# Fused attention and two MLPs on one core: in the last three head pairs, GpSimd forms one of four low parts of the transposed exponentials from an SBUF copy, and late raw weights may lie in weight slots

## The chip, the cores and the metric

One core of a Trainium2 chip runs the whole program. The metric is the device time of one execution in microseconds (us); lower is better. Engine names as in the profile: PE is TensorE (PEld its weight loads), DVE VectorE, ACT ScalarE, POOL GpSimd, SP the queue that issues DMAs.

## The reference

```python
# q, k, v: (4 batches, 8 heads, 576 positions, 64)
scores = (rot(q) @ rot(k).T) / 8
attn = exp(scores - scores.max(-1)); attn /= attn.sum(-1) + 1e-9
x = (attn @ v).transpose(0, 2, 1, 3).reshape(2304, 512)
r = maximum(x @ w_in, 0)                       # w_in 512 x 2048
x = (s * (r * r) + b) @ w_out                  # w_out 2048 x 512
g = x @ w_gate                                 # 512 x 1536
out = (g / (1 + exp(-g)) * (x @ w_val)) @ w_out2
```

The weights arrive as 64-bit floats; the output is float32.

## The kernel before, in words

Matmuls keep float32 precision by splitting both operands into a high part (rounded to fp32r) and a low part (the rest). Three matmuls make one product: high by high, high by low, low by high (L874, L875, L876).

**Attention** runs over 16 head pairs p = 0 to 15. A pair's query axis is cut into nine units u of 128 rows and three thirds y of three units each. For a unit, PE makes scores `ps_s` (L677), DVE the negated maximum `nm` (L680), ACT the exponentials `e` (L684). For a third, PE transposes `e` into PSUM in four parts i = 0 to 3 (`ps_t`, L740; the last, 64 rows high, L743). In each part ACT writes the high half `ph` from PSUM (L748), and DVE the low half as `ps_t - ph` (`pl`, L755; for part 3 the low half lies in rows 64 to 127 of `ph`). PE then multiplies by the values (`ps_av`, L770 with `ph`, L772 with `pl`) and ACT evicts the result to `xr` (L783). POOL splits the values into `vh` (L627 high, L629 low); the second half of a pair's values has to wait until `ps_av` no longer reads the old one.

**MLPs.** Weights come as 512 KB tiles `raw` (SP, L305 and L307). A tile holds two chunks, and each is decoded to float32 by four instructions: `dec` on ACT (L323), then on DVE L326, L329 and L334. ACT rounds the high half `w` (L364), POOL or DVE subtracts for the low half (L371). A decoded `dec` is also stored to DRAM (`up`, L349), since later token blocks read it back (L1141) and combine several pieces on DVE (L1155, L1163) for a product with fewer multiplications (`hb`, `acc`). The first MLP's work on batch 0 begins while the last pairs of attention still run, and fills PE between their matmuls. The decode of its weights lies on the same engines as the attention's splitting.

**Order.** Every instruction is handed to a planner inside the kernel as `op(engine, estimated time, function, priority, needs, tokens taken, tokens given back)`. A token stands for a buffer of a pool. The planner runs a list schedule with these estimates and emits each engine's instructions in that order; on the chip each engine runs its list strictly in order. So one edit of an operation can move others, on all engines. `third(y)` in `pair(p)` emits the parts named above, `load()` and the decode functions the weights. The transposes and the `ps_av` groups keep their own order among themselves (`in_turn`).

Of the kernel before, what the change touches and what calls it, by code (L numbers as in the profile page):

```python
# [8 lines left out]
F32 = mybir.dt.float32  # L9
F32R = mybir.dt.float32r  # L10
U32 = mybir.dt.uint32
AF = mybir.ActivationFunctionType
ALU = mybir.AluOpType
# [139 lines left out]
def t_act(n, psum=True, aps=0):  # L153
    return 0.833e-3 * n + (0.051 if psum else 0.093) + 0.093 * aps


def t_dve(n, aps=0):
    return n / 960.0 + 0.065 + 0.06 * aps
# [6 lines left out]
def t_pool(n):  # L165
    return 2.35e-3 * n + 0.08


def t_pool1(n):
    return 1.1e-3 * n + 0.08  # L170
# [7 lines left out]
def tile_attention_moe_moe(  # L178
# [43 lines left out]
    WU0 = 63  # L222
    WUS = 7
    QP = 11

    sch = Schedule()
    op = sch.op
# [63 lines left out]
    def fetch(key, prio, dep=None, after=(), acq=()):  # L291

        kind, f = key
        src = {"in": w_in, "out": w_out, "gate": w_gate, "val": w_val, "out2": w_out2}[kind]
        wide = src.dtype != F32
        n = 2 if wide else 1
        if wide:
            src = src.bitcast(U32)
        st = {}
        raw_tok = Token("raw")  # L300

        def load():
            st["raw"] = raw = raw_p.tile([128, n * 512], U32 if wide else F32, tag="raw", name="raw")
            if kind in ("out", "out2"):
                nc.sync.dma_start(out=raw, in_=src[f * 128:(f + 1) * 128, :])  # L305
            else:
                nc.sync.dma_start(  # L307
                    out=raw.rearrange("p (k m) -> p k m", k=KD),
                    in_=src[:, f * 128 * n:(f + 1) * 128 * n].rearrange("(k p) m -> p k m", p=128),
                )  # L310

        o = W_ld[key] = sch.dma(n * 262144, load, prio, (dep,), (raw_tok, *acq), after=after, pace=1.5)
        if wide:
            dec_tok = Token("dec", "wb") if kind == "in" and f >= WA // 2 else Token("dec")

            def d0():
                two = st["raw"].rearrange("p (m two) -> p m two", two=2)
                st["low"], st["high"] = two[:, :, 0], two[:, :, 1]
                if dec_tok.pool == "dec":
                    st["t"] = dec_p.tile([128, 512], U32, tag="dec", name="dec")  # L320
                else:
                    st["t"] = late[dec_tok.pool].tile([128, 2, 512], F32R, tag="w", name="dec")[:, 0].bitcast(U32)
                nc.scalar.activation(out=st["t"].bitcast(F32), in_=st["high"].bitcast(F32), func=AF.Copy, scale=2.0 ** -112)  # L323

            def d1():
                nc.vector.tensor_scalar(out=st["t"], in0=st["t"], scalar1=3, scalar2=None, op0=ALU.logical_shift_left)  # L326

            def d2():
                nc.vector.scalar_tensor_tensor(  # L329
                    out=st["t"], in0=st["high"], scalar=0x80000000, in1=st["t"], op0=ALU.bitwise_and, op1=ALU.bitwise_or  # L330
                )

            def d3():
                nc.vector.scalar_tensor_tensor(  # L334
                    out=st["t"], in0=st["low"], scalar=29, in1=st["t"], op0=ALU.logical_shift_right, op1=ALU.bitwise_or
                )
                st["val"] = st["t"].bitcast(F32)

            o = op("act", t_act(512, False), d0, prio, (o,), (dec_tok,))
            o = op("dve", t_dve2(512), d1, prio, (o,), port=True)  # L340
            o = op("dve", t_dve(512), d2, prio, (o,), port=True)
            o = op("dve", t_dve(512), d3, prio, (o,), (), (raw_tok,), port=True)
            end = (dec_tok,)
        else:
            st["val"] = None
            end = (raw_tok,)
        if kind != "out":
            dst = {"in": lambda: w_pair["up", f // 2][f % 2], "gate": lambda: w_pair["gv", f][0], "val": lambda: w_pair["gv", f][1], "out2": lambda: w_last_d[f]}[kind]
            kept[key] = sch.dma(262144, lambda: nc.sync.dma_start(out=dst(), in_=st["raw"] if st["val"] is None else st["val"]), prio, (o,), (), end, pace=1.2)  # L349
        return st, o, end  # L350
# [294 lines left out]
    def pair(p, st):  # L645
# [78 lines left out]
        def third(y, pr):  # L724
# [2 lines left out]
            need, give = [exps[u] for u in us] + [eye_op], [e_tok[u] for u in us]  # L727
            ph_tok, pl_tok = Token("ph"), Token("pl")
            blocks = [(u, kc) for kc in range(4) for u in us]
            done = {}  # L730
            for i in range(4):
                t_tok = Token("t")
                part = blocks[4 * i:4 * i + 4]
                n, rows = (512, 128) if part else (QT, 64)

                def tr(i=i, part=part):
                    ps = st["pt", y, i] = ps_t.tile([128, 512], F32, tag="t", name="ps_t")
                    if part:
                        for z, (u, kc) in enumerate(part):
                            nc.tensor.transpose(ps[:, z * 128:z * 128 + 128], st["e", u][:, kc * 128:kc * 128 + 128], ident)  # L740
                    else:
                        for z, u in enumerate(us):
                            nc.tensor.transpose(ps[0:64, z * 128:z * 128 + 128], st["e", u][:, 512:S], ident)  # L743

                def hi(i=i, n=n, rows=rows):
                    if i == 0:
                        st["ph", y] = ph_p.tile([128, 4 * QT + QT], F32R, tag="ph", name="ph")
                    nc.scalar.activation(out=st["ph", y][0:rows, 512 * i:512 * i + n], in_=st["pt", y, i][0:rows, 0:n], func=AF.Copy)  # L748

                def lo(i=i, n=n, rows=rows):  # L750
                    if i == 0:
                        st["pl", y] = pl_p.tile([128, 4 * QT], F32R, tag="pl", name="pl")
                    c = slice(512 * i, 512 * i + n)
                    dst = st["pl", y][:, c] if rows == 128 else st["ph", y][64:128, c]
                    nc.vector.tensor_tensor(out=dst, in0=st["pt", y, i][0:rows, 0:n], in1=st["ph", y][0:rows, c].bitcast(F32), op=ALU.subtract)  # L755

                o = op("pe", 0.11 * (len(part) or 3), tr, pr + 8 * i, need, (t_tok,), give)
                in_turn(o)
                o = op("act", t_act(n), hi, pr + 8 * i, (o,), (ph_tok,) if i == 0 else ())
                done[i] = op("dve", t_dve(n), lo, pr + 8 * i, (o,), (pl_tok,) if i == 0 else (), (t_tok,))  # L760
            v_tok, tmp = Token("v"), Token("tmp")
            o = None
            spans = ((0, 0, QT),) if y == 0 else ((0, 0, QT // 2), (1, QT // 2, QT)) if y == 1 else ((1, 0, QT),)
# [265 lines left out]
    def x_load_s(i):  # L1029
# [28 lines left out]
        for name, home, kh, th, names, zs in quads:  # L1058
            mine = []
            for o, m, b, s in x_pieces(t0 + QS * th, QS, S):  # L1060
                def ld(home=home, kh=kh, o=o, m=m, b=b, s=s, names=names, zs=zs):
                    if o == 0:
                        take(names, zs)
                    for h in range(2):
                        nc.sync.dma_start(
                            out=half(st[home][h])[:, :, o:o + m].bitcast(F32),
                            in_=x_d[b].rearrange("(k p h) t -> h p k t", h=2, p=128)[h, :, 2 * kh:2 * kh + 2, s:s + m],
                        )
                x = sch.dma(2 * 1024 * m, ld, prio, deps, (*(y for x in names for y in toks[x]), *(v_tok[y] for y in zs)) if o == 0 else (), after=lds[-1:])
                x.dur = 1.1  # L1070
                lds.append(x)
                mine.append(x)
            r_tok = r_toks[name] = Token(*ALL)
            for y, (o, m, b, s) in enumerate(x_pieces(t0 + QS * th, QS, S)):
                def ld(name=name, kh=kh, o=o, m=m, b=b, s=s, y=y, r_tok=r_tok):
                    if y == 0:
                        st["r", name] = flat(r_tok).bitcast(F32)[:, 0:n]
                    for j in range(2):
                        src = r_d[b][2 * kh:2 * kh + 2, S * j + s:S * j + s + m]
                        nc.sync.dma_start(  # L1080
                            out=half(st["r", name])[64 * j:64 * j + 64, :, o:o + m],
                            in_=bass.AP(src.tensor, src.offset, [[0, 64], *(list(x) for x in src.ap)]),
                        )
                x = sch.dma(1024 * m, ld, prio, deps, (r_tok,) if y == 0 else (), after=lds[-1:])
                x.dur = 1.1
                lds.append(x)
                mine.append(x)
            need[name] = mine
# [594 lines left out]
```

## Time and profile before

| | |
|---|---|
| median of 3 runs | 1091.49 us (1089.80 to 1091.75) |
| profiled execution | 1093.18 us, its span 1091.40 us |
| busy, share of the span | PE 1076.0 us (99%), PEld 976.4 (89%), DVE 886.2 (81%), ACT 737.0 (68%), POOL 225.3 (21%) |

The profiled execution has its own time: 1.78 us lie outside the span, and it is 1.69 us above the median of the runs that were timed without a profile. Attention holds the first 289 us of the span; from then on only the MLPs run. A matmul counts as busy until its modelled end, so a high share is not PE at its peak.

### The profile page before, as it was taken

How to read it: one execution, taken by the hardware profiler on the slowest of the kernel's cores; microseconds unless marked ns; L12 is line 12 of the kernel's file. 1: busy time of each engine (PE TensorE's matmuls, PEld its weight loads, DVE VectorE, ACT ScalarE, POOL GpSimd, SP SyncE). 2: the span in 40 equal slices, each digit the busy share in tenths (PEclk: the TensorE clock that was granted, in tenths of full speed). 3: DMA queues.
4: the chain of work that ended last, by engine and by line, in shares of the span. 5: the costliest groups of instructions: out<-in, count | busy, mean ns of one | idle time of the engine just before them, and what ended most of it. 6: DMA issues, size and time to landing. Idle time of an engine off the chain costs nothing.

```text
span 1091.4 us, 17609 instructions
## 1 busy us (share of the span) xinstructions
PE 1076.0 (99%) x6188; PEld 976.4 (89%) x6188; DVE 886.2 (81%) x1560; ACT 737.0 (68%) x1511; POOL 225.3 (21%) x197
## 2 busy tenths in 40 slices
PE   8999999999999999999999999999999999999998
PEld 7899988998888899999888888999989999899996
DVE  6999999999888998879999998876596675966751
ACT  5998999999887876646665556655565554655550
POOL 7898778983210000000000000000000000000000
PEclk8999999999999999999999999999999999999999
DMA  4666868656569555472556654312331122311102
GB/s 124 199 186 226 269 185 260 192 187 206 147 209 271 152 174 174 140 228 88 172 184 202 227 170 148 123 62 65 89 95 39 59 68 80 97 48 45 53 2 57
DMA packets 111192, 155.51 MB, mean 142 GB/s; under 512 B 34416, under 2 KB 67200, under 8 KB 111104
## 3 DMA queue, kind: packets, MB, share of 16 engines
q1 hardware_dynamic: 110288, 153.60, 44.9%
q8 instruction: 49, 0.80, 0.3%
q10 hardware_dynamic: 816, 0.79, 0.2%
q14 instruction: 39, 0.32, 0.1%
HBM read 99.98 MB, written 32.58 MB: 121 GB/s over the span
## 4 chain that ended last, share of the span: by engine, by line
PE 86%; DVE 5%; ACT 4%; DMA 3%; issue 1%; SPq 0%; DVEq 0%; ACTq 0%
PE hb L874 14%; PE hb L876 14%; PE hb L875 14%; PE ps_s L677 6%; PE acc L876 5%; PE acc L875 5%; PE acc L874 5%; PE acc L1465 5%; PE acc L1466 5%; PE acc L1464 5%; PE ps_t L740 4%; PE ps_av L770 3%; PE ps_av L772 2%; DVE nm L680 2%; ACT e L684 1%; DVE pl L755 1%
## 5 line engine op out<-in xcount | busy, mean ns | idle before, releaser
L874 PE MATMUL hb<-w 128*128 128x384 f32 (+1 forms) x728 | 250.9, 345 | 0.0
L876 PE MATMUL hb<-w 128*128 128x384 f32 (+1 forms) x728 | 250.5, 344 | 0.0
L875 PE MATMUL hb<-w 128*128 128x384 f32 (+1 forms) x728 | 250.1, 344 | 0.0
L874 PEld LDWEIGHTS hb<-w 128*128 128x128 f32 x728 | 136.7, 188 | 9.2 <-ACT tmp L1267 0.6
L875 PEld LDWEIGHTS hb<-w 128*128 128x128 f32 x728 | 136.7, 188 | 7.4
L876 PEld LDWEIGHTS hb<-w 128*128 128x128 f32 x728 | 136.7, 188 | 4.6
L680 DVE TENSOR_REDUCE nm<-ps_s 128x1 f32<-128x576 f32 x144 | 107.9, 751 | 9.4 <-PE ps_s L677 7.6
L748 ACT ACTIVATE ph<-ps_t 128x512 fp32r<-128x512 f32 x192 | 106.0, 570 | 11.0 <-PE ps_t L740 9.8
L684 ACT ACTIVATE e<-ps_s,nm 128x576 f32<-128x576 f32 x144 | 107.3, 745 | 8.5 <-DVE nm L680 7.3
L876 PE MATMUL acc<-gh,w 128*128 128x512 f32 (+1 forms) x288 | 106.8, 371 | 0.0
L875 PE MATMUL acc<-gl,w 128*128 128x512 f32 (+1 forms) x288 | 106.7, 370 | 0.0
L874 PE MATMUL acc<-gh,w 128*128 128x512 f32 (+1 forms) x288 | 106.6, 370 | 0.0
L677 PE MATMUL ps_s<-t,a 128*128 128x288 f32 x320 | 100.8, 331 | 4.3 <-ACT e L684 3.7
L770 PE MATMUL ps_av<-ph,vh 128*128 128x384 f32 (+1 forms) x320 | 97.1, 333 | 2.2 <-DVE ph L755 1.3
L755 DVE TENSOR_TENSOR pl<-ps_t,ph 128x512 fp32r<-128x512 f32 x144 | 95.6, 682 | 2.3 <-ACT ph L748 1.0
L1525 ACT ACTIVATE tmp<-hb 128x384 f32<-128x384 f32 x144 | 70.4, 489 | 34.5 <-PE hb L876 32.7
L677 PE MATMUL ps_s<-kz,a 128*128 128x288 f32 x320 | 90.5, 298 | 0.0
L740 PE MATMUL ps_t<-ident,e 128*128 128x128 f32 x576 | 85.9, 274 | 2.9 <-DVE pl L755 1.2
L740 PEld LDWEIGHTS ps_t<-ident,e 128*128 128x128 f32 x576 | 68.6, 141 | 10.0 <-issue 1.7
L1163 DVE TENSOR_TENSOR w<-sums,w 128x512 fp32r<-128x512 f32 x104 | 68.2, 684 | 7.7 <-ACT w L1161 7.5
L772 PE MATMUL ps_av<-pl,vh 128*64 128x384 f32 (+1 forms) x256 | 72.4, 295 | 0.0
L677 PEld LDWEIGHTS ps_s<-t,a 128*128 128x128 f32 x320 | 61.6, 192 | 9.9 <-ACT e L684 8.2
(139 smaller groups left out, 2430.3 us busy)
## 6 DMA issues: line engine op xcount, KB each, us to landing
raw<-gv SPq DMA_DIRECT2D x36, 512.0 KB, 3.7
raw<-in_moe_w_out_dram SPq DMA_DIRECT2D x28, 512.0 KB, 4.6
x_d<-xr SPq DMA_DIRECT2D x64, 144.0 KB, 3.0
raw<-in_moe_w_in_dram SPq DMA_DIRECT2D x16, 512.0 KB, 4.5
raw<-up SPq DMA_DIRECT2D x16, 512.0 KB, 3.9
raw<-in_moe_w_gate_dram SPq DMA_DIRECT2D x12, 512.0 KB, 4.6
raw<-in_moe_w_val_dram SPq DMA_DIRECT2D x12, 512.0 KB, 5.0
gv<-dec SPq DMA_DIRECT2D x24, 256.0 KB, 2.6
```

The costliest lines, as they stand in the source:

```text
L677: nc.tensor.matmul(ps[:, hf * 512:hf * 512 + HS], a[:, q0:q0 + 128], m[:, k0:k0 + HS], start=y == 0, stop=y == len(todo) - 1)
L680: nc.vector.tensor_reduce(out=st["nm"][:, u:u + 1], in_=st["s", u], axis=AX.XY, op=ALU.max, negate=True)
L684: nc.scalar.activation(out=st["e", u].rearrange("p (f n) -> p f n", f=2), in_=st["s", u], func=AF.Exp, bias=st["nm"][:, u:u + 1], accum_ou ...
L740: nc.tensor.transpose(ps[:, z * 128:z * 128 + 128], st["e", u][:, kc * 128:kc * 128 + 128], ident)
L748: nc.scalar.activation(out=st["ph", y][0:rows, 512 * i:512 * i + n], in_=st["pt", y, i][0:rows, 0:n], func=AF.Copy)
L755: nc.vector.tensor_tensor(out=dst, in0=st["pt", y, i][0:rows, 0:n], in1=st["ph", y][0:rows, c].bitcast(F32), op=ALU.subtract)
L770: nc.tensor.matmul(ps, vv, st["ph", y][:, c], start=kc == 0, stop=kc == 4, skip_group_check=True)
L772: nc.tensor.matmul(ps[0:64], vv[:, 0:64], st["pl", y][:, c], start=False, stop=False, skip_group_check=True)
L874: nc.tensor.matmul(o, lh, rh, start=first, stop=False, skip_group_check=more)
L875: nc.tensor.matmul(o, lh, rl, start=False, stop=False, skip_group_check=more)
L876: nc.tensor.matmul(o, ll, rh, start=False, stop=last, skip_group_check=more)
L1525: nc.scalar.activation(out=st[key, f], in_=ps[name], func=AF.Copy)
```

## The change

1. For pairs 13, 14 and 15 (`LP = 13`), part i = 0 of each third (`LC = (0,)`) is split in another way. ACT copies `ps_t` from PSUM to an SBUF tile `raw` (a slot of the later `gl` buffers, token "gb"), and the `ps_t` buffer is given back when that copy ends, not after DVE's subtraction. POOL rounds the copy to `ph` (`hi_p`) and subtracts to `pl` (`lo_p`). DVE's subtraction is left out. These are nine parts of 128x512. The other three parts of a third stay as they were.
2. `raw` tiles of the first MLP's weights with f of at least `WA // 2` may take a slot of the weight buffers ("wb") where no "raw" slot is free.
3. Some loads of a later block carry `pace=1.3` in the planner's account. That alters its estimate, not the transfer.

```diff
+    LP = 13
+    LC = (0,)
...
-        raw_tok = Token("raw")
+        raw_tok = Token("raw", "wb") if kind in ("in", "out") and f >= WA // 2 else Token("raw")
...
-            st["raw"] = raw = raw_p.tile([128, n * 512], U32 if wide else F32, tag="raw", name="raw")
+            if raw_tok.pool == "raw":
+                st["raw"] = raw = raw_p.tile([128, n * 512], U32 if wide else F32, tag="raw", name="raw")
+            else:
+                st["raw"] = raw = late["wb"].tile([128, 2, 512], F32R, tag="w", name="raw").rearrange("p h m -> p (h m)").bitcast(U32)
...
+                def copy(i=i):
+                    if i == 0:
+                        both()
+                    st["raw", y, i] = late["gb"].tile([128, 512], F32R, tag="gl", name="raw").bitcast(F32)
+                    nc.scalar.activation(out=st["raw", y, i], in_=st["pt", y, i], func=AF.Copy)
+
+                def hi_p(i=i):
+                    c = slice(512 * i, 512 * i + 512)
+                    nc.gpsimd.tensor_scalar(out=st["ph", y][:, c], in0=st["raw", y, i], scalar1=1.0, scalar2=0.0, op0=ALU.mult, op1=ALU.add)
+
+                def lo_p(i=i):
+                    c = slice(512 * i, 512 * i + 512)
+                    nc.gpsimd.tensor_tensor(out=st["pl", y][:, c], in0=st["raw", y, i], in1=st["ph", y][:, c].bitcast(F32), op=ALU.subtract)
+
                 o = op("pe", 0.11 * (len(part) or 3), tr, pr + 8 * i, need, (t_tok,), give)
                 in_turn(o)
-                o = op("act", t_act(n), hi, pr + 8 * i, (o,), (ph_tok,) if i == 0 else ())
-                done[i] = op("dve", t_dve(n), lo, pr + 8 * i, (o,), (pl_tok,) if i == 0 else (), (t_tok,))
+                first = (ph_tok, pl_tok) if i == 0 else ()
+                begun = None if i == 0 else act_op[0]
+                if p >= LP and i in LC:
+                    r_tok = Token("gb")
+                    o = act_op[i] = op("act", t_act(n), copy, pr + 8 * i, (o, begun), (*first, r_tok), (t_tok,))
+                    o = op("pool", t_pool1(n), hi_p, pr + 8 * i, (o,))
+                    done[i] = op("pool", t_pool(n), lo_p, pr + 8 * i, (o,), (), (r_tok,))
+                    continue
+                o = act_op[i] = op("act", t_act(n), hi, pr + 8 * i, (o,), first)
+                done[i] = op("dve", t_dve(n), lo, pr + 8 * i, (o,), (), (t_tok,))
...
-                x = sch.dma(2 * 1024 * m, ld, prio, deps, ..., after=lds[-1:])
+                x = sch.dma(2 * 1024 * m, ld, prio, deps, ..., after=lds[-1:], pace=1.3 if i == 1 else 1.0)
```

The lists of all engines are the same up to about 246 us of the profiled execution of before. From there they differ until about 470 us, where PE's list is the same again. The diff adds lines: L684 of before is L689 after, L680 is L685, L748 is L758, L755 is L763, L364 is L369, L371 is L376, L627 and L629 are L632 and L634, L770 and L772 are L800 and L802; L769 is the new copy, L773 and L777 are `hi_p` and `lo_p`.

The first three places are at the start of pair 13's tail, from 246 us on. ACT's list there, before and then after; `w` with `dec` is the rounding of a weight:

```order
L684 ACTIVATE e_3905,l_3470<-ps_s_3861,nm_3730 128x576
L748 ACTIVATE ph_3915<-ps_t_3896 128x512
L684 ACTIVATE e_3925,l_3470<-ps_s_3888,nm_3730 128x576
L748 ACTIVATE ph_3915<-ps_t_3910 128x512
L748 ACTIVATE ph_3915<-ps_t_3929 128x512
L364 ACTIVATE w_3950<-dec_3721 128x512
L783 ACTIVATE xr_3783<-ps_av_3884 128x384
L684 ACTIVATE e_3963,l_3470<-ps_s_3920,nm_3730 128x576
```

```order
L689 ACTIVATE e_3905,l_3470<-ps_s_3861,nm_3730 128x576
L769 ACTIVATE raw_3917<-ps_t_3896 128x512
L689 ACTIVATE e_3927,l_3470<-ps_s_3888,nm_3730 128x576
L758 ACTIVATE ph_3915<-ps_t_3910 128x512
L758 ACTIVATE ph_3915<-ps_t_3931 128x512
L689 ACTIVATE e_3953,l_3470<-ps_s_3922,nm_3730 128x576
L813 ACTIVATE xr_3783<-ps_av_3884 128x384
L758 ACTIVATE ph_3915<-ps_t_3957 64x384
```

The copy to `raw` stands in the place of the first `ph`. The rounding of the weight, which stood ahead of the eviction `xr`, has gone back four rows, and an exponential stands in its place.

DVE's list at the same place, before and then after; `dec` is the decode of a weight:

```order
L680 TENSOR_REDUCE nm_3730<-ps_s_3888 128x1
L334 SCALAR_TENSOR_TENSOR dec_3721<-raw_3286,dec_3721 128x512
L755 TENSOR_TENSOR pl_3937<-ps_t_3896,ph_3915 128x512
L680 TENSOR_REDUCE nm_3730<-ps_s_3920 128x1
L755 TENSOR_TENSOR pl_3937<-ps_t_3910,ph_3915 128x512
L755 TENSOR_TENSOR pl_3937<-ps_t_3929,ph_3915 128x512
L680 TENSOR_REDUCE nm_3730<-ps_s_3944 128x1
```

```order
L685 TENSOR_REDUCE nm_3730<-ps_s_3888 128x1
L339 SCALAR_TENSOR_TENSOR dec_3722<-raw_3287,dec_3722 128x512
L685 TENSOR_REDUCE nm_3730<-ps_s_3922 128x1
L763 TENSOR_TENSOR pl_3916<-ps_t_3910,ph_3915 128x512
L763 TENSOR_TENSOR pl_3916<-ps_t_3931,ph_3915 128x512
L685 TENSOR_REDUCE nm_3730<-ps_s_3946 128x1
```

One subtraction, that of part 0, is gone; the rest has moved up by a row.

POOL's list there, before and after; `vh` is the split of values, `w` the low half of a weight:

```order
L371 TENSOR_TENSOR w_3894<-dec_3613,w_3894 128x512
L627 TENSOR_SCALAR vh_3959<-vr_3636 128x5x64
L371 TENSOR_TENSOR w_3950<-dec_3721,w_3950 128x512
L629 TENSOR_TENSOR vh_3959<-vr_3636,vh_3959 128x5x64
L627 TENSOR_SCALAR vh_4092<-vr_3636 128x5x64
```

```order
L376 TENSOR_TENSOR w_3894<-dec_3613,w_3894 128x512
L773 TENSOR_SCALAR ph_3915<-raw_3917 128x512
L777 TENSOR_TENSOR pl_3916<-raw_3917,ph_3915 128x512
L632 TENSOR_SCALAR vh_3974<-vr_3636 128x5x64
L634 TENSOR_TENSOR vh_3974<-vr_3636,vh_3974 128x5x64
L773 TENSOR_SCALAR ph_3979<-raw_3981 128x512
L777 TENSOR_TENSOR pl_3980<-raw_3981,ph_3979 128x512
L376 TENSOR_TENSOR w_4000<-dec_3722,w_4000 128x512
```

Each copy brings two POOL instructions, and they stand ahead of the next split of values. Over the tail of attention, ACT's list holds nine weight instructions (L323, L364 of before) where it held twelve, and DVE's thirteen decode instructions where it held seventeen; the others come behind it.

SP's list at the end of attention, before and after; `x_d3` and `up` are stores, `raw` loads:

```order
L305 DMA raw_4648<-in_moe_w_out_dram 128x1024
L307 DMA raw_4701<-in_moe_w_in_dram 128x4x256
L349 DMA up3_141<-dec_4698 128x512
L305 DMA raw_4738<-in_moe_w_out_dram 128x1024
L307 DMA raw_4778<-in_moe_w_in_dram 128x4x256
L349 DMA up4_142<-dec_4750 128x512
```

```order
L312 DMA raw_4732<-in_moe_w_in_dram 128x4x256
L310 DMA raw_4740<-in_moe_w_out_dram 128x1024
L312 DMA raw_4746<-in_moe_w_in_dram 128x4x256
L310 DMA raw_4751<-in_moe_w_out_dram 128x1024
L312 DMA raw_4757<-in_moe_w_in_dram 128x4x256
L310 DMA raw_4766<-in_moe_w_out_dram 128x1024
```

Before, a store of a decoded tile stands between every two loads. After, the loads follow one another, eleven in a row, since weight slots take them.

## Rows read from the trace of the kernel before

**Rows 1.** Busy time of each engine in four stretches of the span.

```profile
core 0: us, PE busy (x) PEld busy (x) DVE busy (x) ACT busy (x) POOL busy (x), PEclk, DMA share, GB/s
27.00:246.00 219.00, 214.12 (x1675) 199.11 (x1674) 205.18 (x326) 205.46 (x487) 184.79 (x154) 1.00 0.67 213
246.00:289.00 43.00, 40.60 (x303) 35.83 (x302) 42.06 (x71) 41.05 (x97) 12.85 (x14) 1.00 0.57 173
289.00:379.00 90.00, 90.00 (x408) 73.78 (x408) 79.29 (x124) 72.49 (x124) 7.95 (x6) 1.00 0.70 215
379.00:1064.00 685.00, 684.79 (x3515) 628.29 (x3514) 540.37 (x1007) 400.41 (x767) 0.00 (x0) 1.00 0.35 113
```

**Rows 2.** The chain that ended last, 240 to 292: start, us, engine, line.

```profile
251.56 0.83 ACT e L684 x2
...
266.45 0.67 DVE pl L755
...
285.97 0.55 DVE ph L755
```

**Rows 3.** PE's timeline: start, us, line, tiles, shapes [idle before <-releaser].

```profile
248.04 0.34 PE L677 MATMUL ps_s<-t,a 128*128 128x288 f32 x1
248.21 0.30 PE L677 MATMUL ps_s<-kz,a 128*128 128x288 f32 x1
...
249.94 0.41 PE L770 MATMUL ps_av<-ph,vh 128*128 128x384 f32 x1 [0.65 <-ACT xr L783]
...
286.57 0.44 PE L770 MATMUL ps_av<-ph,vh 128*128 128x384 f32 x1 [0.81 <-DVE ph L755]
```

**Rows 4.** Waits, 246 to 289: us in total, times, longest us.

```profile
PEld ps_s L677 <- ACT e L684: 1.3, 4, 0.5
PEld ps_av L770 <- DVE ph L755: 1.2, 1, 1.2
```

**Rows 5.** Groups of instructions, 246 to 289: count, busy us, mean ns, idle before.

```profile
L755 DVE TENSOR_TENSOR pl<-ps_t,ph 128x512 fp32r<-128x512 f32 x24 | 15.9, 681 | 0.3 <-ACT ph L748 0.2
L748 ACT ACTIVATE ph<-ps_t 128x512 fp32r<-128x512 f32 x25 | 14.3, 594 | 0.9 <-PE ps_t L740 0.9
...
L371 POOL TENSOR_TENSOR w<-dec,w 128x512 fp32r<-128x512 f32 x6 | 7.7, 1283 | 11.5 <-DVE pl L755 7.3 <-ACT w L364 4.2
...
L783 ACT ACTIVATE xr<-ps_av 128x384 f32<-128x384 f32 x8 | 4.0, 496 | 0.1
...
L334 DVE SCALAR_TENSOR_TENSOR dec<-raw,dec 128x512 uint32<-128x512 uint32 x5 | 3.4, 680 | 0.0
...
L364 ACT ACTIVATE w<-dec 128x512 fp32r<-128x512 f32 x5 | 3.2, 638 | 0.3 <-DVE dec L334 0.3
```

**Rows 6.** POOL's groups over the whole run.

```profile
L627 POOL TENSOR_SCALAR vh<-vr 128x320 fp32r<-128x320 f32 x32 | 14.8, 463 | 29.4 <-PE ps_av L770 29.1
L569 POOL TENSOR_SCALAR qkhi<-x 128x384 fp32r<-128x384 f32 x15 | 9.9, 664 | 7.2 <-ACT x L565 7.1
```

**Rows 7.** POOL's timeline at a split of values near 258 us.

```profile
258.24 0.46 POOL L627 TENSOR_SCALAR vh<-vr 128x320 fp32r<-128x320 f32 x1 [6.64 <-PE ps_av L770]
```

**Rows 8.** The timeline from 301 to 305, DVE alone and beside POOL.

```profile
301.40 0.68 DVE L334 SCALAR_TENSOR_TENSOR dec<-raw,dec 128x512 uint32<-128x512 uint32 x1
...
304.16 1.34 POOL L371 TENSOR_TENSOR w<-dec,w 128x512 fp32r<-128x512 f32 x1 [3.22 <-ACT w L364]
...
304.26 1.78 DVE L334 SCALAR_TENSOR_TENSOR dec<-raw,dec 128x512 uint32<-128x512 uint32 x1
```

**Rows 9.** One of DVE's decode groups, 27 to 246.

```profile
L334 DVE SCALAR_TENSOR_TENSOR dec<-raw,dec 128x512 uint32<-128x512 uint32 x5 | 4.0, 793 | 0.0
```

**Rows 10.** First use of read-back weights on DVE and PE; the busy time before it.

```profile
376.45 0.68 DVE L1163 TENSOR_TENSOR w<-raw,w 128x512 fp32r<-128x512 f32 x1
...
379.07 0.33 PE L874 MATMUL hb<-w 128*128 128x384 f32 x1
...
355.00:379.00 24.00, 24.00 (x106) 19.55 (x105) 23.05 (x34) 19.87 (x33) 0.00 (x0) 1.00 0.57 168
```

More of the change, by code (lines that the diff above doesn't have):

```diff
@@ L729, in third, with both @@
             blocks = [(u, kc) for kc in range(4) for u in us]
-            done = {}
+            done, act_op = {}, {}
+            def both():
+                st["ph", y] = ph_p.tile([128, 4 * QT + QT], F32R, tag="ph", name="ph")
+                st["pl", y] = pl_p.tile([128, 4 * QT], F32R, tag="pl", name="pl")
             for i in range(4):
@@ L746, in hi @@
                     if i == 0:
-                        st["ph", y] = ph_p.tile([128, 4 * QT + QT], F32R, tag="ph", name="ph")
+                        both()
                     nc.scalar.activation(out=st["ph", y][0:rows, 512 * i:512 * i + n], in_=st["pt", y, i][0:rows, 0:n], func=AF.Copy)
                 def lo(i=i, n=n, rows=rows):
-                    if i == 0:
-                        st["pl", y] = pl_p.tile([128, 4 * QT], F32R, tag="pl", name="pl")
                     c = slice(512 * i, 512 * i + n)
@@ L755, in lo @@
                     nc.vector.tensor_tensor(out=dst, in0=st["pt", y, i][0:rows, 0:n], in1=st["ph", y][0:rows, c].bitcast(F32), op=ALU.subtract)
+                def copy(i=i):
+                    if i == 0:
+                        both()
+                    st["raw", y, i] = late["gb"].tile([128, 512], F32R, tag="gl", name="raw").bitcast(F32)
[6 more added lines that the diff above has]
+                    nc.gpsimd.tensor_tensor(out=st["pl", y][:, c], in0=st["raw", y, i], in1=st["ph", y][:, c].bitcast(F32), op=ALU.subtract)
                 o = op("pe", 0.11 * (len(part) or 3), tr, pr + 8 * i, need, (t_tok,), give)
                 in_turn(o)
-                o = op("act", t_act(n), hi, pr + 8 * i, (o,), (ph_tok,) if i == 0 else ())
-                done[i] = op("dve", t_dve(n), lo, pr + 8 * i, (o,), (pl_tok,) if i == 0 else (), (t_tok,))
+                first = (ph_tok, pl_tok) if i == 0 else ()
[8 more added lines that the diff above has]
+                done[i] = op("dve", t_dve(n), lo, pr + 8 * i, (o,), (), (t_tok,))
             v_tok, tmp = Token("v"), Token("tmp")
@@ L1068, in ld @@
                         )
-                x = sch.dma(2 * 1024 * m, ld, prio, deps, (*(y for x in names for y in toks[x]), *(v_tok[y] for y in zs)) if o == 0 else (), after=lds[-1:])
+                x = sch.dma(2 * 1024 * m, ld, prio, deps, (*(y for x in names for y in toks[x]), *(v_tok[y] for y in zs)) if o == 0 else (), after=lds[-1:], pace=1.3 if i == 1 else 1.0)
                 x.dur = 1.1
@@ L1083, in ld @@
                         )
-                x = sch.dma(1024 * m, ld, prio, deps, (r_tok,) if y == 0 else (), after=lds[-1:])
+                x = sch.dma(1024 * m, ld, prio, deps, (r_tok,) if y == 0 else (), after=lds[-1:], pace=1.3 if i == 1 else 1.0)
                 x.dur = 1.1
```

## The prediction

> **What bounds the kernel now.** I read the busy time by stretch first, to see where time can be won at all. From 289 us on PE is busy 90.00 of 90 and 684.79 of 685 us [rows 1]. An edit can win nothing there; it can only put something in PE's way. From 27 to 246 the instruction lists of both kernels are the same. That leaves 246 to 289, the tail of attention. There PE is busy 40.60 of 43.00 us, DVE 42.06 and ACT 41.05, POOL 12.85 [rows 1]. DVE and ACT are full and POOL is idle for 30 us. PE's idle time is 2.40 us.
>
> The second view is the chain that ended last. In this stretch it does not run on PE: it lies on ACT from 247 to about 266 us and on DVE from 266 to 288, row after row without a gap (three of the rows in [rows 2]). So both vector engines set the pace in turn, ACT in the first half and DVE in the second.
>
> The third view is PE's timeline, for what ends its stalls. The two longest are a `ps_av` that waits 0.65 us for ACT's eviction `xr`, and a `ps_av` that waits 0.81 us for DVE's last low part [rows 3]. These two make 1.46 of the 2.40 us; the rest is pieces of some tenths. Weight loads wait a little as well, 1.3 us in four pieces for ACT's exponentials and 1.2 us for DVE's low part [rows 4], most of it beneath matmuls that still run.
>
> **DVE's part of the sum.** Nine subtractions of 681 ns leave DVE [rows 5]: 9 x 0.681 = 6.1 us. Four of its seventeen decode instructions move behind the tail as well, at up to 680 ns [rows 5] 2.7 us. DVE's demand in the stretch goes from 42.06 to about 33.3 us, well under PE's 40.60.
>
> **ACT's part.** The copy replaces the rounding of the same PSUM part, 594 ns. The nearest copy from PSUM to SBUF is the eviction `xr`, 496 ns for 384 columns [rows 5]. So it lies between 0.50 and, scaled to 512 columns, 0.66 us: nine times -0.10 to +0.07, or -0.9 to +0.6 us. I take the rounding's 594 ns, since both read as many columns of PSUM in one instruction, and so nothing. Three of twelve weight instructions move behind the tail, by 638 ns each [rows 5] 1.9 us. ACT goes from 41.05 to about 39.1 us, below PE's 40.60, but only by 1.5 us. In the order, the rounding of a weight no longer stands ahead of the `xr` for which PE waited 0.65 us; an exponential stands there in its place, which is no shorter. So this one stall may stay.
>
> **POOL's part.** Each of nine parts adds a rounding and a subtraction. The trace has no 128x512 rounding by POOL. A smaller one bounds it from below, 463 ns for 320 columns; from above, 664 ns for 384 columns scaled to 512 gives 0.89 us [rows 6]. I take 0.74 us, 463 ns scaled by 512/320, since that group is tighter and stands in this stretch. The subtraction has the shape of POOL's weight subtraction, 1.283 us [rows 5]. So 9 x 2.02 = 18.2 us (15.7 to 19.6), and POOL goes from 12.85 to 31 of 43 us. It has the room.
>
> What matters is latency. Before, a first part took 0.594 on ACT and 0.681 on DVE; now 0.594 + 0.74 + 1.283 = 2.62 us and one more hop between engines. That is 1.34 us more, and uncovered it would cost 9 x 1.34 = 12.1 us. The cover is PE's own work. In the changed list, between a third's first transposes and the first `ps_av` that reads them, stand the other transposes of the third, scores of the next units, and MLP matmuls. With the starts of score matmuls 0.17 us apart [rows 3] and the other forms counted likewise, this makes 3.7 us in the tightest third and 4.4 to 6.3 us in seven others. All are longer than 2.62 us. So I cost the latency at nothing. If the copy itself came over 1 us late, the tightest third would lose its cover.
>
> The two instructions stand in POOL's list ahead of value splits, and others stand behind one. The split of values waits up to 6.64 us for `ps_av` to leave the old values [rows 7]. Whatever `hi_p` is queued behind such a split waits with it, and then PE's `ps_av` waits for `hi_p`. In the list the split stands ahead of the third that comes after the one whose `ps_av` frees it, so PE frees it before it needs that part; I cost it at nothing too.
>
> **Weight slots and pace.** Eleven weight loads follow one another on SP at the end of attention where stores stood between them. This removes SP's waits for "raw" slots, and these showed nowhere on PE. The pace changes only the planner's account. Both are 0; a loss can come only from displaced work, see the second rival.
>
> **The sum.** PE can gain no more than its 2.40 us of idle time as the rows show it, and after the change both DVE (33.3) and ACT (39.1) need less than PE's 40.60. I take the whole: 1093.18 - 2.40 = 1090.78 us for the profiled execution. That one stands 1.69 us above the median of the runs, so 1091.49 - 2.4 = 1089.1, rounded to 1089.0. The own range is -1.2 (the stall behind `xr` and half of the short waits stay) to -3.0, so 1088.5 to 1090.3.
>
> **The page's rule against this change.** First the rows. Where a POOL subtraction ran beside a DVE decode instruction, the latter took 1.78 us, alone 0.68 [rows 8]. Yet from 27 to 246, with POOL busy 184.79 of 219 us [rows 1], the mean of that instruction was only 793 ns [rows 9].
> The Trainium skill, page "SBUF — State Buffer", section "SBUF: two separate sides", says that GpSimd and VectorE share a pair of ports as an exclusive lock, taken by whichever starts first for its whole instruction, against a DVE instruction with two SBUF inputs. By it the 1.78 us is one such lock, and the low parts from PSUM that remain on DVE would be free of it, since they have one SBUF input. The trace agrees in the rows just named, and the averages show that it seldom strikes.
> The Trainium skill, page "Perfetto Trace Analysis", section "Optimizing Scalar/DVE Operations", warns that moving work between these two engines might not help for that reason.
>
> **Rivals.**
> *Slower: collisions between POOL and DVE.* POOL is now busy for 31 of 43 us beside thirteen decode instructions in the tail. A collision costs 1.78 - 0.68 = 1.10 us [rows 8]. If all thirteen met one, DVE would need 33.3 + 14.3 = 47.6 us, 4.6 more than the stretch lasted: 1096.1 us. It turns from a gain to a loss at (43 - 33.3) / 1.10, some nine of thirteen. Against it: with POOL busy 84% before, the mean rose by only 0.11 us [rows 5, 9], and 13 x 0.11 is 1.4 us, which DVE has free. Chance 0.09, 1093 to 1096 us.
>
> *No change: the gain is given back.* Four DVE instructions and three of ACT's come later, in the stretch to 379 us. At its end DVE is busy 23.05 of 24 us, and a weight combined for the next block is ready at 377.13 us, 1.94 before its first use at 379.07 [rows 10]. If PE comes 2.4 us earlier and DVE's deferred 2.7 us are still before it, PE waits there and the whole gain is lost. For DVE's chain coming forward speaks that it idles for 10.7 us from 289 to 379 [rows 1]. If it does so in part, 0 to 0.8 us remain gained: 1091.1 us. The same time comes out where ACT, only 1.5 us below PE in the tail, goes on ending PE's stalls. Chance 0.21.
>
> *More than forecast.* The modelled ends hide part of each stall: a score matmul counts 0.34 us, but the next starts after 0.17 [rows 3]. About a dozen waits of PE and of its weight loads would each hold another 0.17, 2.0 us in all, so -4.4 and 1087.1 us. Against it: PE would have to run without any hitch between two engines that are still 77 and 91% busy. Chance 0.08.
>
> **How the numbers follow.** The forecast has 0.62. A measurement of this kernel tells about 0.2%, 2.2 us, from no change. The forecast of -2.4 lies close to that bound, and some six tenths of it fall beyond: 0.37, with the third rival 0.45 for faster. Slower has the first rival's 0.09, and the rest, 0.46, is no change. The range takes half of the third rival and all of the second: 1086.9 to 1091.7.
>
> **What would show it.** In the profile after: POOL rows for the new rounding near 0.74 us and the subtraction near 1.28; DVE some 33 of 43 us in the tail and no longer in the chain; the end of attention 2 us earlier; the `ps_av` that waited for DVE's `ph` gone from the waits. The prediction is wrong if PE waits for POOL's `pl`, if decode instructions stretch beyond 1 us on average, if ACT holds the chain for the whole tail, or if PE stalls anew where the read-back weights are first used.

## The result, and the profile after

The changed kernel takes 1099.34 us, median of 6 runs (1097.65 to 1102.98), against 1091.62 us of before (6 runs, 1089.80 to 1095.40). The ratio is 1.0067, 95% interval 1.0043 to 1.0091: slower by 7.7 us in the medians, where 2.4 us less were forecast and 1091.7 was the end of the range. The profiled execution took 1099.47 us, its span 1097.7 (before 1093.18 and 1091.40).

The busy time by stretch of the changed kernel, columns as in [rows 1]:

```profile
246.00:289.00 43.00, 41.53 (x323) 38.38 (x323) 38.63 (x63) 40.70 (x98) 28.53 (x30) 1.00 0.50 146
289.00:296.00 7.00, 7.00 (x35) 5.86 (x34) 5.24 (x8) 5.89 (x11) 3.18 (x4) 1.00 0.74 257
296.00:379.00 83.00, 76.03 (x319) 61.00 (x318) 67.13 (x102) 57.26 (x97) 7.82 (x6) 0.94 0.68 223
```

The tail went about as forecast: PE's idle time fell from 2.40 to 1.47 us, DVE's busy time from 42.06 to 38.63, POOL is at 28.53. But from 296 to 379, where PE of before was never idle, it now lacks 7 us, and its granted clock is 0.94.

PE's waits from 240 to 1070 name that place:

```profile
PE acc L904 <- ACT gh L960: 7.0, 1, 7.0
PE ps_av L800 <- DVE ph L763: 1.2, 1, 1.2
```

I follow it backwards, in the timelines of PE, ACT and SP of the changed kernel:

```profile
323.24 0.40 PE L906 MATMUL hb<-x,w 128*128 128x512 f32 x1
330.59 0.80 PE L904 MATMUL acc<-gh,w 128*128 128x512 f32 x1 [6.96 <-ACT gh L960]
...
332.42 0.63 PE L904 MATMUL acc<-gh,w 128*128 128x512 f32 x1
```

```profile
319.79 0.63 ACT L953 ACTIVATE r<-r 128x512 f32<-128x512 f32 x1
328.14 0.66 ACT L328 ACTIVATE dec<-raw 128x512 f32<-128x512 f32 x1 [7.71 <-DMA up<-dec]
...
329.93 0.61 ACT L960 ACTIVATE gh<-r 128x512 fp32r<-128x512 f32 x1
```

```profile
309.56 2.13 SPq L354 DMA_DIRECT2D up<-dec  x1
...
316.57 1.94 SPq L310 DMA_DIRECT2D raw<-in_moe_w_out_dram  x1
318.60 0.38 SPq L354 DMA_DIRECT2D up<-dec  x1
```

PE waits for the activation `gh`. ACT's list has a decode instruction ahead of it, and that one needs a free `dec` buffer. The buffer is held by a tile that is still being stored (`up<-dec`). The store was issued at 318.60 and landed 9.5 us later, when ACT's wait ended. Ahead of it in SP's queue stand the row of eleven loads (300.44 to 309.03), one other store (309.56) and five more loads. The issue itself took 0.38 us; some issues of the row took longer, up to 2.15 us for a load and 2.13 for the store at 309.56, where a store's issue usually takes 0.33. How long DMAs took from issue to landing, 300 to 330, changed kernel first, then before:

```profile
raw<-in_moe_w_in_dram SPq DMA_DIRECT2D x8, 512.0 KB, 10.6
...
up<-dec SPq DMA_DIRECT2D x5, 256.0 KB, 9.1
```

```profile
raw<-in_moe_w_in_dram SPq DMA_DIRECT2D x5, 512.0 KB, 4.1
...
up<-dec SPq DMA_DIRECT2D x4, 256.0 KB, 2.6
```

From 300 to 330, SP's queue keeps the 16 DMA engines busy for 92.7% of their time, where it was 62.8% before. So the loads that follow one another fill the DMA engines, and a store that was 2.6 us away is 9.1 us away.

PE's clock adds to it. Behind the wait the matmuls start 0.43 us apart (331.99, 332.42, 332.85), where the same matmuls elsewhere are 0.23 apart. The granted clock of 330 to 340 is 0.68, the lower of the two levels (1.2 GHz) for part of it, after PE had stood idle for 7.0 us:

```profile
330.00:340.00 10.00, 9.39 (x28) 7.13 (x29) 8.78 (x15) 6.98 (x14) 0.00 (x0) 0.68 0.07 27
```

To add up, I take the same matmul of PE's list in both traces, since starts differ by up to 3 us between executions. Before, then after, the last transposes ahead of the first difference and one MLP matmul behind attention:

```profile
248.79 0.49 PE L743 MATMUL ps_t<-ident,e 128*64 128x128 f32 x3
...
298.81 0.39 PE L874 MATMUL hb<-x,w 128*128 128x512 f32 x1
```

```profile
247.98 0.49 PE L753 MATMUL ps_t<-ident,e 128*64 128x128 f32 x3
...
296.07 0.39 PE L904 MATMUL hb<-x,w 128*128 128x512 f32 x1
```

This execution was 0.81 us ahead before anything differs, and 2.74 us ahead behind attention: the tail won 1.93 us. The matmul at 330.59 stands at 326.24 in the trace of before, so there it is 4.35 us behind: the wait cost 7.09. A matmul of the next block's `hb` starts at 385.87 before and at 393.16 after, 7.29 behind; the 2.9 us more are lost within 6 us of the wait's end, at the low clock. The span ends 6.3 us later; the last microsecond comes back in pieces up to 600 us, which I did not follow.

### The profile page after: what moved, and what is told of

It is laid out like the page before. It is cut to its first block, busy times and chain, and to the rows that moved or that the text cites. A ratio compares the mean times of both kernels' runs of the same rounds, so it can differ in the third digit from the quotient of the medians.

```text
span 1097.7 us, 17627 instructions
## 1 busy us (share of the span) xinstructions
PE 1076.7 (98%) x6188; PEld 979.2 (89%) x6188; DVE 883.5 (80%) x1551; ACT 734.4 (67%) x1511; POOL 244.7 (22%) x215
## 4 chain that ended last, share of the span: by engine, by line
PE 90%; ACT 3%; DVE 3%; DMA 2%; issue 1%; SPq 0%; DVEq 0%; ACTq 0%
PE hb L904 14%; PE hb L906 14%; PE hb L905 14%; PE ps_s L682 7%; PE acc L905 5%; PE acc L904 5%; PE acc L906 5%; PE ps_t L750 5%; PE acc L1496 5%; PE acc L1494 5%; PE acc L1495 5%; PE ps_av L800 4%; PE ps_av L802 3%; PE ps_t L753 1%; PE pst L555 1%
## 5 line engine op out<-in xcount | busy, mean ns | idle before, releaser
L685 DVE TENSOR_REDUCE nm<-ps_s 128x1 f32<-128x576 f32 x144 | 108.0, 752 | 11.2 <-PE ps_s L682 9.4
L689 ACT ACTIVATE e<-ps_s,nm 128x576 f32<-128x576 f32 x144 | 107.3, 745 | 7.6 <-DVE nm L685 6.9
L758 ACT ACTIVATE ph<-ps_t 128x512 fp32r<-128x512 f32 (+1 forms) x183 | 101.2, 570 | 11.3 <-PE ps_t L750 10.1
L800 PE MATMUL ps_av<-ph,vh 128*128 128x384 f32 (+1 forms) x320 | 97.2, 333 | 2.1 <-DVE ph L763 1.6
L763 DVE TENSOR_TENSOR pl<-ps_t,ph 128x512 fp32r<-128x512 f32 x135 | 89.8, 683 | 3.6 <-ACT ph L758 1.9
L1193 DVE TENSOR_TENSOR w<-sums,w 128x512 fp32r<-128x512 f32 x104 | 68.3, 685 | 8.5 <-ACT w L1191 8.3
L802 PE MATMUL ps_av<-pl,vh 128*64 128x384 f32 (+1 forms) x256 | 72.2, 295 | 0.0
```

The lines of the kernel that those rows point to most:

```text
L685: nc.vector.tensor_reduce(out=st["nm"][:, u:u + 1], in_=st["s", u], axis=AX.XY, op=ALU.max, negate=True)
L689: nc.scalar.activation(out=st["e", u].rearrange("p (f n) -> p f n", f=2), in_=st["s", u], func=AF.Exp, bias=st["nm"][:, u:u + 1], accum_ou ...
L800: nc.tensor.matmul(ps, vv, st["ph", y][:, c], start=kc == 0, stop=kc == 4, skip_group_check=True)
L802: nc.tensor.matmul(ps[0:64], vv[:, 0:64], st["pl", y][:, c], start=False, stop=False, skip_group_check=True)
```

## The experiments

Each version was timed beside the kernel before; it has five runs where the text gives no other number. Theory A says that the weight slots make the row of loads, and this the late store; B that the GpSimd split pushes decode work behind the tail and this is what PE waits for; C that the DMA engines are full, wherever the store is issued.

**The split without the slots.**

```diff
-        raw_tok = Token("raw", "wb") if kind in ("in", "out") and f >= WA // 2 else Token("raw")
+        raw_tok = Token("raw")
```

> This is the changed kernel with its second part undone: raw weight tiles lie in raw slots only, the GpSimd split of pairs 13 to 15 and the pace stay. Theory A (the slots let a long row of 512 KB loads into the DMA queue, a store of a decoded tile lands behind it, the decode buffer stays taken, and ACT and then PE wait): no row of loads, no PE wait over 1 us after 290 us, and only the tail's gain is left, 1.9 us of the changed profile, so a ratio near 0.998 (1088.5 to 1090.8 where before takes 1091.6). Rival B (the GpSimd part pushes decode instructions behind the tail, and these are what PE waits for): the wait of 7 us stays, ratio 1.005 or more.

1099.15 us, ratio 1.0065 (1.0052 to 1.0078). Neither theory: the wait near 323 is gone, as A said, but another 7 us are lost in the trace near 384, where the read-back weights of the next block are first used. PE, and behind it DVE ahead of that place:

```profile
384.05 0.44 PE L904 MATMUL hb<-w 128*128 128x384 f32 x1 [1.99 <-ACT w L1191]
```

```profile
378.98 0.95 DVE L1122 TENSOR_TENSOR w<-w 128x768 f32<-128x768 f32 x1
...
383.44 0.95 DVE L1134 TENSOR_TENSOR w<-w 128x768 fp32r<-128x768 f32 x1
...
384.64 0.68 DVE L1193 TENSOR_TENSOR w<-raw,w 128x512 fp32r<-128x512 f32 x1
```

Six instructions that form the next block's operands (L1122, L1134) stand in DVE's list ahead of the first combination L1193. The clock takes its part here too: PE waits 1.99 and 0.71 us, and from 384.7 to 391.5 its granted clock is 0.50. This is the place of the prediction's second rival.

**The slots alone** (no split, no pace).

```diff
-    LP = 13
+    LP = 99
...
-                x = sch.dma(2 * 1024 * m, ..., after=lds[-1:], pace=1.3 if i == 1 else 1.0)
+                x = sch.dma(2 * 1024 * m, ..., after=lds[-1:])
...
```

> This is the changed kernel without the GpSimd split and without the pace: only the second part, raw tiles in weight slots. Theory A: loads stand in rows of eight and nine on SP, a store lands 8 us or more after its issue, PE waits 5 to 9 us for the first MLP's activations near 320 us and its clock falls to the lower level behind the wait; with no gain in the tail the time is 1098 to 1103 us, ratio 1.006 to 1.010. Rival B: no wait, ratio 1.000 within 0.001.

1093.61 us (11 runs), ratio 1.0015 (1.0003 to 1.0026). The row of loads and the late store are there: nine loads follow one another from 306.56 on, and the store behind them lands after 9.2 us. SP's timeline, and ACT's waits from 289 to 384:

```profile
315.94 2.16 SPq L310 DMA_DIRECT2D raw<-in_moe_w_out_dram  x1
318.20 0.38 SPq L354 DMA_DIRECT2D up<-dec  x1
```

```profile
ACT dec L328 <- DMA up<-dec: 2.9, 1, 2.9
```

But ACT waits 2.9 us for it, not 7.7, and PE has no wait over 0.4 us after 289. The jam is due to the slots, as A says; that it costs 7 us is not due to them alone.

**The stores on ACT's queue**, every list otherwise that of the changed kernel.

```diff
-            kept[key] = sch.dma(262144, lambda: nc.sync.dma_start(out=dst(), ...
+            q = nc.scalar if kind == "in" and f >= 6 else nc.sync
+            kept[key] = sch.dma(262144, lambda: q.dma_start(out=dst(), ...
```

> The changed kernel with every engine's order kept, but the stores of decoded tiles from the seventh on are issued from ACT's queue in place of SP's. Theory A in its narrow form (the store stands behind the loads in one queue): the stores land within 6 us, the wait shrinks below 2 us, and the time is 1089 to 1092 us less up to 0.5 us per store that ACT issues, at most 1094. Rival C (the 16 DMA engines are full with the loads, so a store is late from whichever queue): the wait stays above 5 us and the time at 1097 to 1101 us. Rival B: no change against the changed kernel.

1091.51 us (12 runs), ratio 0.9996 (0.9986 to 1.0005): 8 us less than the changed kernel, and no PE wait over 0.4 us after 290. Issue to landing, 300 to 330:

```profile
raw<-in_moe_w_out_dram SPq DMA_DIRECT2D x8, 512.0 KB, 9.5
...
up<-dec ACTq DMA_DIRECT2D x5, 256.0 KB, 6.3
```

The loads are nearly as slow as in the changed kernel (9.5 and 8.9 us, where they took 9.5 and 10.6), and the DMA engines as full (354 GB/s, where they moved 334), but the stores pass them. So C falls: what cost the time was the place behind the loads in SP's queue. The Trainium skill, page "DMA: Bandwidth & Descriptors", section "Queues, rings and completion order", says that SP and ACT each have their own ring on the same DMA engines, which serve the rings in turn; the trace agrees, 6.3 against 9.1 us. The section "Issuing engines are not separate DMA queues" of the Trainium skill's same page says of issuing from several engines that it only saves the time to issue. Here it saved 8 us of the kernel's time, and the measurement decides.

**The low half on DVE**, from the SBUF copy; GpSimd only rounds; no slots.

```diff
-                    nc.gpsimd.tensor_tensor(out=st["pl", y][:, c], in0=st["raw", y, i], ...
+                    nc.vector.tensor_tensor(out=st["pl", y][:, c], in0=st["raw", y, i], ...
-                    done[i] = op("pool", t_pool(n), lo_p, pr + 8 * i, (o,), (), (r_tok,))
+                    done[i] = op("dve", t_dve(n), lo_p, pr + 8 * i, (o,), (), (r_tok,))
```

> As the first run (no weight slots for raw tiles), but the low half of the nine parts is subtracted by DVE from the SBUF copy; GpSimd only rounds. PSUM is given back early as in the change, DVE's load is as before. If the tail's gain comes from DVE's relief, it is gone: ratio 1.000 within 0.0012. If it comes from the earlier release of the transposes' buffer, it stays: ratio near 0.998.

1099.09 us, ratio 1.0070 (1.0055 to 1.0085). The loss near 384 us, which the first run has too, hides what was asked. In the trace DVE is full again in the tail:

```profile
246.00:289.00 43.00, 41.68 (x307) 37.01 (x306) 42.12 (x67) 40.05 (x93) 17.08 (x20) 1.00 0.50 157
```

Between the two matmuls named above, the trace of this run has 49.65 us, the first run's 49.42, that of before 50.02. I call it inconclusive on the source of the gain.

**A bounded row of loads**: the slots stay, but a load may go only after the store of the tile three before it.

```diff
-        weight(..., sw0, lo_eng="pool" if z < WA + 6 else "dve")
+        weight(..., sw0, lo_eng="pool" if z < WA + 6 else "dve", after=[kept["in", z // 2 - 3]] if z // 2 >= 3 + 5 else ())
```

> The changed kernel, but each load of a weight tile may be issued only after the store of the tile three before it was issued: weight slots still take raw tiles, the weights come no later than in the changed kernel's list, but at most four loads stand in a row. If the store behind the row of loads is the cause of the wait near 323 us, and late last weights are the cause of the loss near 384 us without the slots, both are gone: no PE wait over 1 us after 290 us, and the tail's gain of 1.9 us is left: ratio 0.997 to 0.999, 1088.5 to 1090.7 us. If the split itself costs time that the tail does not show, the ratio is 1.003 or more.

1090.36 us (11 runs, 1087.81 to 1097.76), ratio 0.9997 (0.9980 to 1.0013). Both waits are gone; the longest PE wait behind 289 is 0.4 us. Issue to landing, 300 to 330:

```profile
raw<-in_moe_w_in_dram SPq DMA_DIRECT2D x5, 512.0 KB, 4.7
up<-dec SPq DMA_DIRECT2D x5, 256.0 KB, 2.5
```

A second cure that leaves the split, the slots and the pace in place, so the store behind the row of loads is what the slow-down needs. The gain of 1.9 us stands in the trace (from 246.00 to 294.07 for the pair of matmuls at 248.79 and 298.81 before: 48.07 against 50.02 us), but the time is not measurably shorter than before.

**The split alone, without slots and pace.** Edits as in the first two.

> GpSimd split alone: no weight slots for raw tiles and no pace of 1.3 on the later block's loads. If the loss near 384 us in the first run comes from weights that are late (raw slots hold them back while the split pushes decode instructions behind the tail), it stays whatever the pace: ratio 1.004 to 1.008. If it comes from where the pace puts the later block's loads, it is gone: ratio 0.998 to 0.9995.

1093.31 us (11 runs), ratio 1.0013 (1.0000 to 1.0027). So the 7 us near 384 us of the first run hang on the pace. In DVE's timeline the first combination now stands ahead of the last operands:

```profile
379.03 0.68 DVE L1193 TENSOR_TENSOR w<-raw,w 128x512 fp32r<-128x512 f32 x1
...
382.38 0.95 DVE L1134 TENSOR_TENSOR w<-w 128x768 fp32r<-128x768 f32 x1
```

**Two of four parts to GpSimd**, bounded row.

```diff
-    LC = (0,)
+    LC = (0, 2)
...
-                o = act_op[i] = op("act", t_act(n), hi, pr + 8 * i, (o,), first)
+                o = act_op[i] = op("act", t_act(n), hi, pr + 8 * i, (o, begun if p >= LP else None), first)
```

The second edit lets ACT's work on a later part of a third go only after that on its first part.

> As the bounded row, but two of the four parts of each third (the first and the third) go to GpSimd in pairs 13 to 15: DVE is relieved of another 6.1 us, GpSimd gets another 18 us and is then busy for nearly all of the tail. If DVE still sets the pace, another 0.5 to 1.5 us are won against the bounded row. If ACT does, or if GpSimd becomes the limit, it is equal or up to 3 us slower than that.

1102.61 us, ratio 1.0099 (1.0078 to 1.0120). In the trace 8.7 of the 10.0 us are lost in the tail, between the same two matmuls (58.69 us, before 50.02). POOL is busy for 38.11 of 43 us, PE for 38.08, and PE waits for the PSUM buffers of the transposes:

```profile
246.00:289.00 43.00, 38.08 (x276) 34.73 (x275) 36.29 (x50) 37.05 (x88) 38.11 (x40) 0.96 0.48 148
```

```profile
PE ps_t L753 <- ACT raw L769: 3.4, 1, 3.4
PE ps_t L750 <- DVE pl L763: 3.0, 2, 2.8
```

**The bounded row without the split** (`LP = 99`).

> The bounded row of loads without the GpSimd split (the pace stays): what the split is worth is the difference to the bounded row with it. If the split's worth is the tail's gain, this is 1.9 us slower than the bounded row: ratio 0.999 to 1.001 against the kernel before.

1092.28 us (11 runs), ratio 1.0005 (0.9994 to 1.0015). From 246.55 to 296.61 the same pair of matmuls takes 50.06 us, against 50.02 before: without the split nothing is won in the tail.

**The changed kernel without the pace.**

> The changed kernel without the pace: GpSimd split and weight slots together. The row of eleven loads stands in its list too. If the split and the slots together make the wait (each alone costs under 0.2%, since the slots alone leave the decode enough reserve), the wait of some 7 us near 323 us stays: ratio 1.005 to 1.009. If it needed the pace as well, the ratio is 0.998 to 1.002.

1101.68 us (6 runs), ratio 1.0082 (1.0062 to 1.0103), PE's wait 6.6 us. Split and slots together make it.

**The split from pair 12 on**, bounded row (`LP = 12`, and the second edit of the run with two parts).

> The bounded row with the GpSimd split from pair 12 on, twelve parts in place of nine. If DVE's relief wins time wherever DVE is full and POOL free, another 0.3 to 1 us are gained against the bounded row (ratio 0.996 to 0.9985). Before 246 us POOL is busy for 84% of the time with the rotation of later pairs: if that has no room for a third as much again, it is 1 to 4 us slower.

1094.55 us (12 runs), ratio 1.0025 (1.0012 to 1.0038): slower. The same pair of matmuls takes 51.93 us, so the tail loses 1.9 us where it gained. From 220 to 246, ahead of it, POOL is nearly full; that this is the reason was not tried by itself:

```profile
220.00:246.00 26.00, 25.33 (x202) 23.64 (x201) 22.64 (x35) 24.49 (x59) 24.58 (x25) 1.00 0.54 152
```

**The bounded row without the pace.**

> The bounded row with the split, without the pace. If the pace only matters where weights are late (as without the slots), there is no difference to the bounded row with it: ratio 0.997 to 1.0005. If the pace costs or gives by itself, the difference stands in the trace between 340 and 480 us.

1092.08 us (12 runs), ratio 0.9997 (0.9985 to 1.0009), as with the pace.

## Why the prediction was wrong

**The step that failed** is the one on weight slots and pace: "Both are 0; a loss can come only from displaced work". It read SP's waits for "raw" slots as idle time that nobody misses. They were the spacing that kept the stores of decoded tiles close behind the loads. The order shown ahead of the prediction has the eleven loads in a row, and that the store's end frees the decode buffer stands in the code; what was not asked is how long a store takes behind them. In one queue with them it takes 9.1 us in place of 2.6. The pace was not nothing either: with the split and no slots it makes the loss near 384 us (1.0065 with it, 1.0013 without).

**Why it costs 7 us only with the split.** The slots alone make the same jam and cost 0.15%, the split alone 0.13%, both 0.82% (0.67% with the pace). The store is equally late in both (9.5 and 9.2 us), and ACT's list shows what differs. By the matmul behind attention that served above (298.81 in the trace of before), ACT has begun 12 decodes `dec` with the split and 14 without. The decode that needs the late store's buffer is the 21st with the split, and it stands ahead of the sixth `gh`, the one that PE waits for. With the slots alone it is the 24th, and the sixth `gh` has started 4.7 us before it:

```profile
322.83 0.64 ACT L960 ACTIVATE gh<-r 128x512 fp32r<-128x512 f32 x1
...
327.49 0.66 ACT L328 ACTIVATE dec<-raw 128x512 f32<-128x512 f32 x1 [2.93 <-DMA up<-dec]
```

With the same split and the store on time (the bounded row), the 21st decode also stands ahead of the sixth `gh`, starts at 319.16, and PE does not wait. So the slots make the store late, and with the split it holds up the `gh` that PE needs next. Why the late buffer falls to the 21st decode with the split and to the 24th without it was not followed. Theory B is right in so far as the split is needed, wrong in that it does not make the wait.

**DVE's part** was right in kind and oversized: 38.63 us where 33.3 were forecast. The stretch holds only six subtractions of 128x512 fewer (18 for 24) and two decode instructions fewer (13 for 15): before, attention's last three such subtractions lie behind 289 us, up to 292, and what is left of them now lies within the stretch. So the forecast took nine subtractions from a stretch that held eight of them. The two long decode instructions also take 768 and 727 ns in place of some 680. DVE now idles 4.4 us in the stretch. The chain that ended last shows that the mechanism was right: from 246 to 289 it lay on DVE for 21.6 us and on ACT for 14.8 before, and lies on PE for 37.6 us now.

**ACT's part** held in the price of the copy, 598 ns against 602 of the rounding, and was oversized in the sum: ACT is busy for 40.70 us where 39.1 were forecast. The stall behind `xr` near 249 us is gone, and the longest one left, 1.2 us, is for DVE's `ph`; I had expected the first to stay and the second to go.

**POOL's part** held. Groups of the changed kernel, 246 to 296:

```profile
L777 POOL TENSOR_TENSOR pl<-raw,ph 128x512 fp32r<-128x512 f32 x9 | 12.4, 1382 | 0.8
...
L773 POOL TENSOR_SCALAR ph<-raw 128x512 fp32r<-128x512 f32 x9 | 6.6, 732 | 8.4 <-ACT raw L769 8.3
```

732 and 1382 ns, where 0.74 and 1.283 us were taken; 28.5 us busy, where 31 were. No matmul waited for it.

**The tail's gain**, forecast 2.40, was 1.93 us in three traces with the split (the changed kernel, the stores on ACT, the bounded row: 1.91 to 1.95) and only some 0.6 in four others (0.56 to 0.62), though the kernel without the pace has the same lists here as the changed one. The first rival's collision tells the two outcomes apart. POOL and DVE in the changed kernel without the pace, and then in the changed kernel itself:

```profile
270.06 1.29 POOL L777 TENSOR_TENSOR pl<-raw,ph 128x512 fp32r<-128x512 f32 x1
```

```profile
270.08 1.81 DVE L339 SCALAR_TENSOR_TENSOR dec<-raw,dec 128x512 uint32<-128x512 uint32 x1
```

```profile
272.02 1.85 POOL L777 TENSOR_TENSOR pl<-raw,ph 128x512 fp32r<-128x512 f32 x1
```

```profile
272.05 0.68 DVE L339 SCALAR_TENSOR_TENSOR dec<-raw,dec 128x512 uint32<-128x512 uint32 x1
```

The same two instructions begin within 0.03 us of each other in both. In all four traces with the small gain DVE's takes 1.81 us, another of DVE's decode instructions 6 us later takes 1.55 to 1.56 (0.42 in the changed kernel), and PE waits 0.7 to 0.8 us for a score buffer four microseconds later; in the three with the large one POOL's takes 1.85 or 1.86, and PE does not wait. The Trainium skill, page "SBUF — State Buffer", section "SBUF: two separate sides", has the rule, one of the two is shut out for the other's whole instruction; the trace agrees (0.68 alone, 1.81 shut out). The rival's price per collision, 1.10 us, was right (1.81 - 0.68 = 1.13), its number was not: two DVE instructions held for 1.1 us each, not nine, go with 1.3 us less gain. That they cause it is read from the traces; no run tried it.

**The second rival**, the gain given back at the read-back weights, came true without the slots, and its price was far too low: 7 us in place of at most the gain. I took DVE's deferred 2.7 us as the delay. What decided was the list: with the pace, six operand instructions stand ahead of the combination.

**What stays open.** With the jam cured in two ways, the kernel is at 0.9996 and 0.9997 of before: the trace's gain does not show in the time. The tail's smaller outcome in a part of the executions, and 0.6 us that these two traces lose again near 390 us, point to less than 0.1%, which eleven or twelve runs don't tell from nothing. Part of the spread goes with the granted clock: of 23 runs of the kernel before, the five with a mean of 1.000 took 1090.67 us (median), the four with 0.995 took 1093.68. A fit of the time by version and mean clock, made afterwards, puts the two cures 0.7 (plus or minus 0.7) and 1.2 us (plus or minus 1.0) below before: a hint, since a change can alter the clock too. No version measured beats the kernel before beyond its interval.

## What to carry to other kernels

Before a buffer limit is lifted, ask what its waits kept apart: a load that starts earlier goes ahead of stores in the same queue, and if a store's end frees a buffer, the limit can come back there, later and longer. Where a scheduler's lists decide, an edit of one stage has to be read to the end of the region in which the lists differ, each DMA behind the moved ones counted with what waits for it. And work moved to an idle engine that shares something with the full one can pay by chance: the same lists gave 1.9 or 0.6 us.

## What the runs showed of the hardware

A store's time to landing depended on the queue that it stood in, with the same DMA engines full in both: behind 512 KB loads 9.1 us from SP's, 6.3 from ACT's. In the row of loads, an issue on SP took up to 2.15 us, and 0.33 us elsewhere. A row of the profile that merges several issues holds the waits between them as well: the four stores from 318.60 to 334.56 us took 0.32 to 0.38 us each, and in between SP waited up to 12.2 us for DVE.

Two instructions on POOL and DVE that began within 0.03 us of each other ended with either one held: DVE for 1.81 us in place of 0.68, or POOL for 1.85 in place of 1.29.

Executions with the same lists reach 246 us up to 3 us apart (the bounded row's trace is 2.79 us ahead of that of before there), so a gain of 2 us is read between matching instructions, not from spans. Most of that lead goes with the clock at the start: from 15 to 22 us the granted clock of before is 0.51, mostly the lower level, after PE was busy for 8.39 of 10 us; from 16 to 22 that of the bounded row is 1.00, after 8.77 of 10. By 69 us the bounded row is 2.1 us ahead.
